# PSUM banks dealt out anew, and weights fetched ahead of their split, in an attention and gated-MLP kernel

## The chip, the cores and the metric

The kernel runs on one core of one Trainium2 chip. The metric is device time in microseconds. Three runs of the kernel before gave 1259.15 us in the median (1252.94 to 1259.8).

## The reference

```
phi(x) = exp(h - max(h)) / sqrt(m),   h = x @ omega.T - sum(x*x)/2      (x scaled by D**-0.25)
kv  = phi(k).T @ v                z = sum over s of phi(k)
x   = (phi(q) @ kv) / (phi(q) @ z + 1e-6)        per batch and head; 8 x 8 heads, 576 rows, D = 64, m = 128
x   -> [4608, 512]                               heads side by side
g   = x @ w_gate;  val = x @ w_val               [4608, 1536] each
out = (silu(g) * val) @ w_out                    [4608, 512]
```

The inputs are float32 (the weights come as 8-byte floats and are converted in the kernel).

## The kernel before, in words

**Precision.** Every matrix of the second half (the MLP, "MoE" in the names) is split into a rounded part and a remainder (`hi` and `lo`, `whi` and `wlo`). A product is three matmuls: hi x hi, hi x lo, lo x hi. ScalarE (ACT) writes the rounded part, VectorE (DVE) or GpSimd (POOL) the remainder.

**Attention, in steps.** 72 steps, each with two groups of 256 rows for a pair of heads (at first keys only, then one query and one key group, at the end two query groups). What a step n does, by function, with the tile that each writes:

- `st_transpose(n + 1)`: four TensorE transposes of the loaded rows `nat` into the PSUM tile `pt` (L373); POOL squares `nat` into `sq` (L380); ACT copies `pt` to `x` (L381).
- `st_project(n)`: `x` times omega into two PSUM tiles `pp`, one for each head of the pair (L396).
- `st_max(n)`: DVE sums the squares (L407), takes the two maxima over `pp` (L414) and makes the bias in two small instructions (L416, L417). The sums are taken ahead of time, some three steps before the maxima of the same step, but stand in the same queue.
- `st_exp(n)`: eight ACT exponentials from `pp` with that bias into `ph` (L428).
- `k_accumulate`: `ph` times `v` into `kvacc` (L530). `q_transpose`: four transposes of a query's `ph` into `ptq` (L554), copied by ACT to `qt` (L556). `q_mult` (batches 0 to 3): `qt` times kv into `po` (L571), normalised by DVE. `q_out`: the result into the PSUM tile `xt` (L604 by transposes, L611 by matmuls), from where ACT copies it, either as `xo` to DRAM (L626) or as the MLP's `xh` with the remainder `xl` by DVE (L632, L633).

**The order of the work.** A list of functions is called for each step: `CLOSE` for steps 0 to 24, `GROUPED` for 25 to 75. Where `GROUPED` has `SHARE`, a stretch of the MLP's work is put in, and of the conversion of the weights (`convert_all`: five DVE instructions for each of 36 pieces, L265 to L273, tiles `st` and `wc`). A scheduler then orders the instructions of each engine by its own estimate of times; each engine and the DMA queue (SP) work strictly in the order that it fixed.

**PSUM.** Eight banks: pool `ps_m` has 4 (MLP tiles `g`, `v`, `o`, and some of the early attention), `ps_p` 2 (`pp`, and besides them `pt` and `xt`), `ps_a` 1 (`ptq`, `po`, `zp`) and `ps_k` 1 (`kvacc`). In the grouped steps `pt` of step n + 1 thus takes the bank that `pp` of step n leaves, and that is free when the exponentials have read it. After attention the last four become `ps_w`, with 4 banks.

**The MLP.** Tiles 0 to 2 (512 rows each) go through `stream()` beside attention: for three columns at a time gate (`g`, L647), SiLU by ACT (L708), value (`v`, L647), product by DVE (L724), split by ACT (`hh`, L727) and POOL (`hl`, L728), down (`o`, L656), added up in `acc` (L671 ACT, L674 DVE). Tiles 3 to 8 go through `pair_rounds()` after it, two tiles at once with seven products in place of eight (Strassen's scheme): 18 visits, each of 2 x 7 products of six matmuls (L851) with eight downs of six matmuls between them. Products are added up in the PSUM tiles `a`, `c`, `d` of `ps_w`, and ACT copies in between (`late`, L919) and DVE sums (L923) stand between products of one tile. New weights come for most visits: `load_seven` fetches two raw pieces (`wraw`, three buffers) from the DRAM scratch `wscr` (L822), DVE forms four sums `s` (L827 to L830), ACT and POOL split them (L841, L842); `load_weights` does it for the down weights (L297, L245, L246). Both start the fetch and the split at the same place of the program.

Of the kernel before, what the change touches and what calls it, by code (L numbers as in the profile page):

```python
# [11 lines left out]
F32 = mybir.dt.float32  # L12
# [11 lines left out]
def kernel(  # L24
# [11 lines left out]
    nc = tc.nc  # L36
# [46 lines left out]
    moe = ctx.enter_context(tc.tile_pool(name="moe", bufs=2))  # L83
    accp = ctx.enter_context(tc.tile_pool(name="accp", bufs=12))
    dram = ctx.enter_context(tc.tile_pool(name="dram", bufs=1, space=DRAM))
    ps_m = ctx.enter_context(tc.tile_pool(name="ps_m", bufs=4, space=PSUM))
    late = ExitStack()
    att = late.enter_context(tc.tile_pool(name="att", bufs=2))
    ps_p = late.enter_context(tc.tile_pool(name="ps_p", bufs=2, space=PSUM))
    ps_a = late.enter_context(tc.tile_pool(name="ps_a", bufs=1, space=PSUM))  # L90
    ps_k = late.enter_context(tc.tile_pool(name="ps_k", bufs=1, space=PSUM))

    ident = const.tile([P, P], F32, name="ident")
# [1 line left out]

    def ps_att(name, shape):
        return ps_a.tile(shape, F32, name=name, tag="b")

    def ps_proj(name, shape):
        return ps_p.tile(shape, F32, name=name, tag="pp")  # L100
# [189 lines left out]
        while (f, i) not in converted:  # L290
            tick()

    def load_weights(f, i, pool=None, tag=None):
        need(f, i)
        new_weights(f, i, pool, tag)
        raw = moe.tile([P, DM], F32, name=f"wraw{f}_{i}", tag="wraw", bufs=3)
        nc.sync.dma_start(raw, wscr[f, i])  # L297
        split_piece(f, i, raw)

# [66 lines left out]
    def st_transpose(n):  # L366
        if n >= NS:
            return
        nat = nats.pop(n)
        pt = (ps_moe if n <= EARLY else ps_proj)(f"pt_{n}", [P, 2, G])  # L370
        for i in range(2):
            for c in range(CH):
                nc.tensor.transpose(  # L373
                    pt[:, i, c * P : (c + 1) * P], nat[:, i, c].rearrange("p h d -> p (h d)"), ident
                )
# [4 lines left out]
        nc.gpsimd.tensor_tensor(sq, nat, nat, op=ALU.mult)  # L380
        nc.scalar.copy(x, pt)  # L381
        sts[n] = x, st, sq
        return True
# [161 lines left out]
    def q_transpose(n):  # L545
        m = n
        todo = [(b, g) for _, b, g, gr in slots(n - TLAG, "q") if b < BPOOL]
        todo += [(b, g) for _, b, g, gr in slots(n - NLAG, "q") if b >= BPOOL]
        for b, g in todo:
            ph = box.pop(("q", b, g))  # L550
            pt = (ps_moe if m < EARLY else ps_att)(f"ptq{b}_{g}", [P, 2, G])
            for hh in range(2):
                for c in range(CH):
                    nc.tensor.transpose(pt[:, hh, c * P : (c + 1) * P], ph[:, c, hh * M : (hh + 1) * M], ident)  # L554
            qts[b, g] = att.tile([P, 2, G], F32, name=f"qt{b}_{g}", tag="qt")
            nc.scalar.copy(qts[b, g], pt)  # L556

    def q_mult(n):
# [36 lines left out]

    def q_out(n):
        n -= OLAG
        for _, b, g, gr in slots(n, "q"):
            po = (ps_att if n + OLAG < EARLY else ps_proj)(f"xt{b}_{g}", [P, G])
            first = column(b, gr)  # L600
            if b < BPOOL:
                xn = xns.pop((b, g))
# [80 lines left out]
    def stream():  # L683

        todo = []
        for vi, (j, s_, k_) in enumerate(visits):
# [24 lines left out]
                for f in fs:  # L711
                    load_weights(nxt[1] * FA + f - fs[0], 0)
            if final:
                load_seven((0, 0), 0)
            while todo:
                down(*todo.pop(0))
                yield MM2
# [12 lines left out]
                if new_set:  # L730
                    load_weights(nxt[1] * FA + f - fs[0], 1)
            if final:
                load_seven((0, 0), 1)
            wts = {f: weights[f, 2] for f in fs} if vi else None
            then = range(nxt[1] * FA, nxt[1] * FA + FA) if new_set else (0, 1) if final else None
            todo = [(j, k_, ht, wts, then, tt) for tt in range(w // P)]
        yield from pair_rounds(todo)

# [76 lines left out]
    def load_seven(key, i):  # L815

        win = late_pools["win"]
        raws_ = []
        r, pf = key
        for f in (2 * pf, 2 * pf + 1):  # L820
            raw = moe.tile([P, DM], F32, name=f"wraw{f}_{i}_{r}", tag="wraw", bufs=3)
            nc.sync.dma_start(raw, wscr[f, i])  # L822
            raws_.append(raw)
# [37 lines left out]
    def pair_rounds(todo):  # L861
# [20 lines left out]
        def one_down():  # L882
            next(prep, None)
            if todo:
                down(*todo.pop(0))
                return True

        for vi, (r, k_, pf) in enumerate(pair_visits):
            then = pair_visits[vi + 1] if vi + 1 < len(pair_visits) else None
            new_w = then and then[2] != pf  # L890
# [18 lines left out]
            for i, use in ((0, gate), (1, value)):  # L909
# [15 lines left out]

                a, c, d = (ps_w.tile([P, T], F32, name=f"{e}{vi}_{i}", tag="w") for e in "acd")
                for n in ORDER:
                    product({5: c, 3: c, 2: d}.get(n, a), n, wts, n in (1, 5, 2))
                    if n == 1:
                        copy("m1", a)  # L930
# [34 lines left out]
    def give(us):  # L965
# [115 lines left out]
```

## Time and profile before

| what | value |
|---|---|
| median of three runs | 1259.15 us |
| the profiled execution's own time | 1259.16 us |
| its span in the trace | 1257.4 us |
| mean granted TensorE clock | 0.973 |
| first matmul of the pairs' visits | 692.7 us after the start of the span |

In the views, PE is TensorE's matmuls and PEld its weight loads. A row of the waits reads "engine and line that waited <- engine and line that ended it: us in total, times, longest". A row of the order of time reads "start, duration, engine, line, operation, out<-in, count [idle before it <- what ended it]". A row of windows gives for each stretch the busy time of each engine with the number of its instructions, then the granted clock and the DMA's share. A step is named by its `pp`: step 47 begins with the projections `pp_47`.

### The profile page before, as it was taken

What the parts mean: (1) busy time and instruction counts of PE and PEld (TensorE: products, weight loads), DVE (VectorE), ACT (ScalarE), POOL (GpSimd) and SP (SyncE); (2) the same over time, 40 slices, a digit from 0 to 9 for tenths busy, and PEclk for the clock granted to TensorE, in tenths of its full rate; (3) what the DMA queues carried; (4) which work ended last, traced back from release to release, by engine and by line L of the source; (5) the groups of instructions that cost most, each with busy time, mean ns of one, the idle gap of its engine ahead of it and who ended that gap; (6) DMA issues with size and microseconds to landing.
All of it is one profiled execution on the core that took longest, in us unless ns stands there. A gap on an engine that the chain in (4) does not pass through costs nothing. (4 is left out here: it accounts for less than half of the span.)

```text
span 1257.4 us, 19064 instructions
## 1 busy us (share of the span) xinstructions
PE 1184.7 (94%) x6633; PEld 968.2 (77%) x6633; DVE 718.8 (57%) x1338; ACT 670.2 (53%) x1503; POOL 608.3 (48%) x515
## 2 busy tenths in 40 slices
PE   6999999989899798998999889999999999999998
PEld 5888777867778576675778778888778888888886
DVE  4788776363765748545527454555744546535544
ACT  3878774656566465465634444444454444454431
POOL 3343333241645747457524456663556662555641
PEclk7999998999899998999999999999999999999999
DMA  5556545352453435222034411112411220412102
GB/s 144 139 141 148 153 132 158 90 151 72 121 140 101 127 92 146 65 73 72 23 111 115 132 62 51 51 51 77 117 42 51 59 60 17 109 51 58 53 17 68
DMA packets 173968, 114.33 MB, mean 91 GB/s; under 512 B 125840, under 2 KB 144304, under 8 KB 173872
## 3 DMA queue, kind: packets, MB, share of 16 engines
q1 hardware_dynamic: 173872, 113.11, 33.0%
q8 instruction: 53, 0.87, 0.3%
q14 instruction: 43, 0.35, 0.1%
HBM read 87.88 MB, written 25.18 MB: 90 GB/s over the span
## 5 line engine op out<-in xcount | busy, mean ns | idle before, releaser
L428 ACT ACTIVATE ph<-pp,st 128x128 f32<-128x128 f32 x576 | 158.3, 386 | 76.2 <-DVE st L417 75.9
L380 POOL TENSOR_TENSOR sq<-nat 128x512 f32<-128x512 f32 x72 | 78.4, 1089 | 141.4 <-DMA nat<-in_k_dram 82.2
L674 DVE TENSOR_TENSOR acc<-o,acc 128x512 f32<-128x512 f32 x156 | 106.6, 684 | 69.8 <-PE o L656 69.8
L842 POOL TENSOR_TENSOR wlo<-wraw,whi 128x512 fp32r<-128x512 f32 (+1 forms) x64 | 66.8, 1043 | 120.5 <-ACT whi L841 119.9
L842 POOL TENSOR_TENSOR wlo<-s,whi 128x512 fp32r<-128x512 f32 x64 | 95.9, 1515 | 57.9 <-ACT whi L841 21.1
L414 DVE TENSOR_REDUCE st<-pp 128x4 f32<-128x512 f32 x144 | 93.6, 683 | 40.9 <-PE pp L396 40.7
L396 PE MATMUL pp<-omT,x 64*128 64x128 f32 x1152 | 102.4, 299 | 1.2 <-ACT x L381 0.4
L396 PEld LDWEIGHTS pp<-omT,x 64*128 64x128 f32 x1152 | 85.0, 198 | 20.9 <-issue 5.4
L246 POOL TENSOR_TENSOR wlo<-wraw,whi 128x512 fp32r<-128x512 f32 x59 | 76.8, 1305 | 40.0 <-ACT whi L245 39.9
L827 DVE TENSOR_TENSOR s<-wraw 128x256 f32<-128x256 f32 x32 | 24.6, 768 | 112.2 <-DMA wraw<-wscr 71.6
L407 DVE TENSOR_REDUCE st<-sq 128x8 f32<-128x512 f32 x72 | 49.1, 681 | 69.0 <-POOL sq L380 69.0
L373 PE MATMUL pt<-ident,nat 128*128 128x128 f32 x288 | 50.9, 299 | 39.1 <-ACT ph L428 36.7
L275 POOL TENSOR_TENSOR wc<-st,wc 128x512 f32<-128x512 f32 x36 | 48.2, 1340 | 73.5 <-DVE wc L273 59.9
L373 PEld LDWEIGHTS pt<-ident,nat 128*128 128x128 f32 x288 | 35.4, 151 | 52.5 <-ACT ph L428 44.5
L656 PE MATMUL o<-whi,late 128*128 128x512 f32 x192 | 74.5, 389 | 0.0
L530 PE MATMUL kvacc<-v,ph 128*128 128x65 f32 x512 | 70.6, 279 | 3.8 <-ACT ph L428 3.3
L530 PEld LDWEIGHTS kvacc<-v,ph 128*128 128x128 f32 x512 | 66.9, 201 | 6.3 <-ACT ph L428 3.6
L919 ACT COPY late<-a 128x512 f32<-128x512 f32 x72 | 42.0, 583 | 50.0 <-PE a L851 47.2
L841 ACT CAST whi<-wraw 128x512 fp32r<-128x512 f32 (+1 forms) x64 | 32.9, 514 | 63.9 <-PE a L851 47.5
L490 POOL TENSOR_TENSOR jk<-ph,zt 128x512 f32<-128x512 f32 x32 | 42.0, 1316 | 48.6 <-ACT ph L428 44.0
L647 PE MATMUL g<-xh,whi 128*128 128x512 f32 x144 | 61.7, 428 | 0.0
L647 PE MATMUL v<-xh,whi 128*128 128x512 f32 x144 | 61.5, 427 | 0.0
(250 smaller groups left out, 3406.0 us busy)
## 6 DMA issues: line engine op xcount, KB each, us to landing
wraw<-wscr SPq DMA_DIRECT2D x123, 256.0 KB, 2.6
wscr<-wc SPq DMA_DIRECT2D x36, 256.0 KB, 2.3
out_dram<-acc SPq DMA_DIRECT2D x72, 128.0 KB, 2.3
nat<-in_k_dram SPq DMA_DIRECT2D x64, 128.0 KB, 3.0
v<-in_v_dram SPq DMA_DIRECT2D x64, 128.0 KB, 3.0
nat<-in_q_dram SPq DMA_DIRECT2D x64, 128.0 KB, 2.6
st<-in_moe_w_gate_dram SPq DMA_DIRECT2D x12, 512.0 KB, 4.9
st<-in_moe_w_val_dram SPq DMA_DIRECT2D x12, 512.0 KB
```

The costliest lines, as they stand in the source:

```text
L246: nc.gpsimd.tensor_tensor(lo, raw, hi.bitcast(F32), op=ALU.subtract)
L373: nc.tensor.transpose(pt[:, i, c * P : (c + 1) * P], nat[:, i, c].rearrange("p h d -> p (h d)"), ident)
L380: nc.gpsimd.tensor_tensor(sq, nat, nat, op=ALU.mult)
L396: nc.tensor.matmul(pp[hh][:, i, c, :], x[r, i, c * P : (c + 1) * P], omT[r], start=True, stop=True)
L407: nc.vector.tensor_reduce(st[:, 0].rearrange("p i c h -> p (i c h)"), sq.rearrange("p i c h d -> p (i c h) d"), axis=AX.X, op=ALU.add,)
L414: nc.vector.tensor_reduce(st[:, 1, :, :, hh], pp[hh], axis=AX.X, op=ALU.max, negate=True)
L428: nc.scalar.activation(ph[:, c, hh * M : (hh + 1) * M], pp[hh][:, i, c, :], AF.Exp, bias=st[:, 3, i, c, hh : hh + 1], scale=1.0,)
L530: nc.tensor.matmul(acc[:, 2 * (pr % 2) + hh, :], ph[:, c, hh * M : (hh + 1) * M], vt[:, 2 * c + j if gr is None else c, hh, :], start=firs ...
L647: nc.tensor.matmul(ps, a_[:, ws], b_[:, c, :], start=n == 0, stop=n == 3 * NC - 1)
L656: nc.tensor.matmul(ps, a_[:, ts_], b_, start=first and n == 0, stop=last and n == 2)
L674: nc.vector.tensor_tensor(a_, po, a_, op=ALU.add)
L842: nc.gpsimd.tensor_tensor(lo, src_, hi.bitcast(F32), op=ALU.subtract)
```

## The change

PSUM: `ps_m` goes from 4 banks to 3, a new pool `ps_b` of one bank takes `pt`, the first `xt` of a step and the second `ptq` of a step; the second `xt` goes to `ps_a`; `ps_p` is left to `pp`. In `GROUPED`, `q_out` moves up behind the first half of `k_accumulate`. `qt` has four buffers in place of two. `ps_w` has five banks. In the pairs' visits a function `weights_work` is called ahead of each product: it fetches (`fetch`) at one product and splits (`make_seven`, or `new_weights` and `split_piece`) at a later one.

```diff
-    ps_m = ctx.enter_context(tc.tile_pool(name="ps_m", bufs=4, space=PSUM))
+    ps_m = ctx.enter_context(tc.tile_pool(name="ps_m", bufs=3, space=PSUM))
...
+    ps_b = late.enter_context(tc.tile_pool(name="ps_b", bufs=1, space=PSUM))
...
+    def ps_tr(name, shape):
+        return ps_b.tile(shape, F32, name=name, tag="t")
...
-        pt = (ps_moe if n <= EARLY else ps_proj)(f"pt_{n}", [P, 2, G])
+        pt = ps_tr(f"pt_{n}", [P, 2, G])
...
-            pt = (ps_moe if m < EARLY else ps_att)(f"ptq{b}_{g}", [P, 2, G])
+            pt = (ps_moe if m < EARLY else ps_tr if i else ps_att)(f"ptq{b}_{g}", [P, 2, G])
...
-            qts[b, g] = att.tile([P, 2, G], F32, name=f"qt{b}_{g}", tag="qt")
+            qts[b, g] = att.tile([P, 2, G], F32, name=f"qt{b}_{g}", tag="qt", bufs=4)
...
-            po = (ps_att if n + OLAG < EARLY else ps_proj)(f"xt{b}_{g}", [P, G])
+            po = (ps_att if n + OLAG < EARLY or i else ps_tr)(f"xt{b}_{g}", [P, G])
...
+        def weights_work(vi, u):
+            r, k_, pf = pair_visits[vi]
+            prev = pair_visits[vi - 1][2] if vi else None
+            fs = (2 * pf, 2 * pf + 1)
+            out_at = 9 if vi == 0 else 2
+            if u == 1 and 1 in coming:
+                make_seven((r, pf), 1, coming.pop(1))
+            if u == out_at and pf != prev:
+                coming[2] = fetch(fs, 2)
+            if u == out_at + 2 and 2 in coming:
+                for f, raw in zip(fs, coming.pop(2)):
+                    new_weights(f, 2, *((accp, "acc") if f % 4 == 3 else ()))
+                    split_piece(f, 2, raw)
+            if vi + 1 < len(pair_visits) and pair_visits[vi + 1][2] != pf:
+                r2, _, pf2 = pair_visits[vi + 1]
+                for i, at in ((0, 5), (1, 12)):
+                    if u == at:
+                        coming[i] = fetch((2 * pf2, 2 * pf2 + 1), i)
+                if u == 8:
+                    make_seven((r2, pf2), 0, coming.pop(0))
...
                 for n in ORDER:
+                    weights_work(vi, unit[0])
+                    unit[0] += 1
                     product({5: c, 3: c, 2: d}.get(n, a), n, wts, n in (1, 5, 2))
...
-                        if new_w:
-                            load_seven((then[0], then[2]), i)
...
-            if new_w:
-                for f in (2 * then[2], 2 * then[2] + 1):
-                    load_weights(f, 2, *((accp, "acc") if f % 4 == 3 else ()))
...
         lambda n: k_accumulate(n, 0),
+        q_out,
         lambda n: k_accumulate(n, 1),
...
-        q_out,
         q_mult,
...
-        ("ps_w", tc.tile_pool(name="ps_w", bufs=4, space=PSUM)),
+        ("ps_w", tc.tile_pool(name="ps_w", bufs=5, space=PSUM)),
```

**TensorE, grouped step 47.** Before, from the last projection of step 47 to the first of step 48 (twelve matmuls for `v_4` and eleven for `v_5` are cut to their first):

```order
L396 MATMUL pp_47_4249<-omT,x_4216 128x128
L554 MATMUL ptq_3_4258<-ident,ph_45_4069 128x128 x4
L530 MATMUL kvacc_1_4059<-v_99,ph_45_4074 128x65 x4
L647 MATMUL v_4_4296<-xh_1236,whi_1_3251 128x512
...
L647 MATMUL v_5_4338<-xh_1236,whi_1_3320 128x512
L373 MATMUL pt_4316<-ident,nat_4026 128x128 x4
L611 MATMUL xt_2_4326<-qt_2_4169,kvr_1_3495 64x256 x2
L647 MATMUL v_5_4338<-xl_1237,whi_1_3320 128x512
...
L396 MATMUL pp_48_4355<-omT,x_4321 128x128
```

The same stretch of TensorE's queue in the changed kernel, whose line numbers are 11 higher here:

```order
L407 MATMUL pp_47_4252<-omT,x_4225 128x128
L565 MATMUL ptq_3_4261<-ident,ph_45_4078 128x128 x4
L541 MATMUL kvacc_1_4068<-v_102,ph_45_4083 128x65 x2
L622 MATMUL xt_2_4270<-qt_2_4172,kvr_1_3507 64x256 x2
L541 MATMUL kvacc_1_4068<-v_102,ph_45_4083 128x65 x2
L658 MATMUL v_4_4305<-xh_1239,whi_1_3256 128x512
...
L384 MATMUL pt_4325<-ident,nat_4029 128x128 x4
L658 MATMUL v_5_4341<-xh_1239,whi_1_3331 128x512
...
L407 MATMUL pp_48_4358<-omT,x_4330 128x128
```

`xt` has moved from behind `pt` to ahead of the MLP's matmuls; the MLP's work between `pt` and the next projections is now a whole group of twelve. On ACT the copy `xo` has moved with `xt`, from behind the exponentials of a step to ahead of them:

```order
L392 COPY x_4225<-pt_4220 128x512
L738 CAST hh_3_4301<-sl_3_4094 128x512
L567 COPY qt_3_4266<-ptq_3_4261 128x512
L637 COPY xo_2_4_4273<-xt_2_4270 128x256
L439 ACTIVATE ph_47_4283<-pp_47_4251,st_4226 128x128 x2
```

Before it read, at the same place of ACT's queue:

```order
L381 COPY x_4216<-pt_4211 128x512
L626 COPY xo_1_4_4224<-xt_1_4221 128x256
L727 CAST hh_3_4292<-sl_3_4085 128x512
L556 COPY qt_3_4263<-ptq_3_4258 128x512
L428 ACTIVATE ph_47_4274<-pp_47_4248,st_4217 128x128 x2
```

So `xo_1` stood behind `x`, and `xo_2` now stands ahead of `ph_47`.

**The DMA queue (SP), first visits of the pairs.** Before, with `wraw_0`, `wraw_1`, `wraw_2` for gate, value and down weights and `out_dram` for finished rows of tile 2:

```order
L297 DMA wraw_2_7663<-wscr 128x512
L678 DMA out_dram<-acc_1_3548 64x512 x2
L678 DMA out_dram<-acc_2_3596 64x512 x2
L822 DMA wraw_1_0_7730<-wscr 128x512
L822 DMA wraw_1_0_7732<-wscr 128x512
L297 DMA wraw_2_7757<-wscr 128x512
```

In the changed kernel:

```order
L307 DMA wraw_2_7678<-wscr 128x512
L689 DMA out_dram<-acc_1_3560 64x512 x2
L689 DMA out_dram<-acc_2_3599 64x512 x2
L307 DMA wraw_1_7715<-wscr 128x512
L307 DMA wraw_1_7717<-wscr 128x512
L307 DMA wraw_2_7789<-wscr 128x512
```

The fetches stand at the same places of the queue as before, in the same order.

More of the change, by code (lines that the diff above doesn't have):

```diff
@@ L291, in need, with load_weights, fetch @@
             tick()
-    def load_weights(f, i, pool=None, tag=None):
+    def load_weights(f, i):
         need(f, i)
[L295 to L298, printed above, removed]
+        fetched = fetch((f,), i)
+        new_weights(f, i)
+        split_piece(f, i, fetched[0])
+    def fetch(fs, i):
+        raws_ = []
+        for f in fs:
+            raw = moe.tile([P, DM], F32, name=f"wraw{f}_{i}", tag="wraw", bufs=3)
+            nc.sync.dma_start(raw, wscr[f, i])
+            raws_.append(raw)
+        return raws_
     omT = const.tile([P, M], F32, name="omT")
@@ L548, in q_transpose @@
         todo += [(b, g) for _, b, g, gr in slots(n - NLAG, "q") if b >= BPOOL]
-        for b, g in todo:
+        for i, (b, g) in enumerate(todo):
             ph = box.pop(("q", b, g))
-            pt = (ps_moe if m < EARLY else ps_att)(f"ptq{b}_{g}", [P, 2, G])
+            pt = (ps_moe if m < EARLY else ps_tr if i else ps_att)(f"ptq{b}_{g}", [P, 2, G])
             for hh in range(2):
@@ L597, in q_out @@
         n -= OLAG
-        for _, b, g, gr in slots(n, "q"):
-            po = (ps_att if n + OLAG < EARLY else ps_proj)(f"xt{b}_{g}", [P, G])
+        for i, b, g, gr in slots(n, "q"):
+            po = (ps_att if n + OLAG < EARLY or i else ps_tr)(f"xt{b}_{g}", [P, G])
             first = column(b, gr)
@@ L713, in stream @@
             if final:
-                load_seven((0, 0), 0)
+                make_seven((0, 0), 0, fetch((0, 1), 0))
             while todo:
@@ L732, in stream @@
             if final:
-                load_seven((0, 0), 1)
+                make_seven((0, 0), 1, fetch((0, 1), 1))
             wts = {f: weights[f, 2] for f in fs} if vi else None
-            then = range(nxt[1] * FA, nxt[1] * FA + FA) if new_set else (0, 1) if final else None
+            then = range(nxt[1] * FA, nxt[1] * FA + FA) if new_set else None
             todo = [(j, k_, ht, wts, then, tt) for tt in range(w // P)]
@@ L813, in split_x, with make_seven @@
         nc.vector.tensor_tensor(lo, ahead[name], hi.bitcast(F32), op=ALU.subtract)
-    def load_seven(key, i):
+    def make_seven(key, i, raws_):
         win = late_pools["win"]
-        raws_ = []
         r, pf = key
[L820 to L823, printed above, removed]
         (a11, a12), (a21, a22) = ((x[:, 0:G], x[:, G:DM]) for x in raws_)
@@ L886, in one_down @@
                 return True
+        coming = {}
+        def weights_work(vi, u):
[18 more added lines that the diff above has]
+                    make_seven((r2, pf2), 0, coming.pop(0))
         for vi, (r, k_, pf) in enumerate(pair_visits):
+            unit = [0]
             then = pair_visits[vi + 1] if vi + 1 < len(pair_visits) else None
-            new_w = then and then[2] != pf
             new_x = then and then[0] != r
```

## The prediction

> **What bounds the kernel now.** I read the page, then windows by stage, then TensorE's waits, then one step in order of time.
>
> ```profile
> span 1257.4 us, 19064 instructions
> PE 1184.7 (94%) x6633; PEld 968.2 (77%) x6633; DVE 718.8 (57%) x1338; ACT 670.2 (53%) x1503; POOL 608.3 (48%) x515
> ```
>
> TensorE is busy 94% of the span and no other engine above 77%, so a gain has to come out of the 73 us in which TensorE stands still, or out of time at a lower clock. The windows show where that is:
>
> ```profile
> core 0: us, PE busy (x) PEld busy (x) DVE busy (x) ACT busy (x) POOL busy (x), PEclk, DMA share, GB/s
> 212.00:640.00 428.00, 388.29 (x2449) 304.55 (x2450) 237.79 (x477) 247.85 (x615) 221.32 (x190) 0.94 0.36 99
> 640.00:692.70 52.70, 52.70 (x255) 42.83 (x254) 29.66 (x44) 22.49 (x40) 15.96 (x13) 1.00 0.42 117
> 692.70:745.00 52.30, 45.23 (x189) 36.01 (x188) 29.43 (x42) 23.68 (x43) 28.72 (x23) 0.97 0.35 103
> 745.00:1240.00 495.00, 492.83 (x2172) 407.04 (x2171) 260.24 (x402) 228.61 (x400) 258.64 (x202) 1.00 0.20 55
> ```
>
> The grouped steps (212 to 640) lose 39.7 us to waits at a clock of 0.94; in the pairs' visits 7.1 us go in the first 52 us and 2.2 us in the next 495. The waits of TensorE, first from 132 to 640 us, then (the last three rows) from 640 us on:
>
> ```profile
> PE pt L373 <- ACT ph L428: 36.7, 20, 4.5
> ...
> PE a L851 <- ACT late L919: 4.9, 3, 3.5
> PE a L851 <- DVE sl2k L923: 2.6, 1, 2.6
> PE o L656 <- POOL hl1k L907: 1.0, 1, 1.0
> ```
>
> One line carries the grouped stage: the transposes `pt` of the next step wait for the exponentials of this one, because they take a bank that `pp` holds. Step 47 in order of time shows what the exponentials wait for:
>
> ```profile
> 368.19 1.16 PE L396 MATMUL pp<-omT,x 64*128 64x128 f32 x16
> 369.28 0.62 SPq L331 DMA_DIRECT2D nat<-in_k_dram  x1
> 369.38 1.29 DVE L414 TENSOR_REDUCE st<-pp 128x4 f32<-128x512 f32 x2 [0.28 <-PE pp L396]
> 371.99 1.04 POOL L380 TENSOR_TENSOR sq<-nat 128x512 f32<-128x512 f32 x1 [0.89 <-DMA nat<-in_k_dram]
> 373.06 0.69 DVE L407 TENSOR_REDUCE st<-sq 128x8 f32<-128x512 f32 x1 [1.93 <-POOL sq L380]
> 373.66 0.16 DVE L417 SCALAR_TENSOR_TENSOR st<-st 128x8 f32<-128x8 f32 x1
> 373.92 2.17 ACT L428 ACTIVATE ph<-pp,st 128x128 f32<-128x128 f32 x8 [3.35 <-DVE st L417]
> 375.62 0.66 PE L373 MATMUL pt<-ident,nat 128*128 128x128 f32 x4 [1.81 <-ACT ph L428]
> 376.37 0.59 ACT L381 COPY x<-pt 128x512 f32<-128x512 f32 x1 [0.29 <-PE pt L373]
> ```
>
> The projections end at 369.35 and the maxima at 370.67, but the bias is held to 373.66 by a sum of squares (L407) that belongs to a step three ahead, whose rows were still on their way. The exponentials end at 376.09, 6.7 us behind the projections. TensorE had reached `pt` 4.5 us behind them and waited 1.81 us.
>
> **The change, part by part.**
>
> *`pt` off the bank of `pp`.* The exponentials still have to be done before the next projections, which need `pp`'s banks, and the copy `x` still stands behind them on ACT. So the wait doesn't vanish: it moves from `pt` to the next `pp`, behind more work. What that is worth, in step 47: before, `pt` (0.66 us in its row; I take 0.44, since the next matmul starts before the last has drained), `xt` (about 0.3, an estimate) and eleven MLP matmuls came after the released wait. The MLP's pitch comes from the chain of waits:
>
> ```profile
> 917.32 1.36 PE c L851 x6
> ```
>
> Six in 1.36 us are 0.227 each, so eleven are 2.5 us, and 3.24 us of TensorE's work now run ahead of the wait. Against it, `pt` could start 0.47 us before the exponentials ended (375.62 against 376.09), and `x` (0.59 us, and about 0.1 to be handed on) now comes after them on the path: 1.16 us. The net cover is 2.1 us per wait. The five longest of the 20 waits are
>
> ```profile
> 281.13 1.11 PE L373 MATMUL pt<-ident,nat 128*128 128x128 f32 x4 [4.54 <-ACT ph L428]
> 336.23 1.11 PE L373 MATMUL pt<-ident,nat 128*128 128x128 f32 x4 [3.24 <-ACT ph L428]
> 440.39 0.66 PE L373 MATMUL pt<-ident,nat 128*128 128x128 f32 x4 [4.03 <-ACT ph L428]
> 483.35 0.90 PE L373 MATMUL pt<-ident,nat 128*128 128x128 f32 x3 [4.24 <-ACT ph L428]
> 584.69 0.69 PE L373 MATMUL pt<-ident,nat 128*128 128x128 f32 x2 [2.93 <-ACT ph L428]
> ```
>
> Less 2.1 each, 2.4 + 1.1 + 1.9 + 2.1 + 0.8 = 8.3 us are left; the other 15, 17.7 us together, leave next to nothing. In the steps of the first and the third, ACT's changed queue has a table load and a SiLU ahead of `x`:
>
> ```profile
> 281.61 1.28 ACT L708 ACT_TABLE_LOAD   x1
> 673.87 0.59 ACT L708 ACTIVATE sl<-g 128x512 f32<-128x512 f32 x1
> ```
>
> That is 1.87 us twice, 3.7 us. I add 2 us (an estimate) for steps where fewer MLP matmuls stood behind `pt`. So 14 us of waits stay and **22.7 us go**. Bounds: 36.7 us if the exponentials come no later and `x` is never late, none if they fall back by the 2.1 us that are gained.
>
> *The clock.* In ten stretches of the grouped stage the granted clock is 0.50. Asked as windows, the one behind step 47's wait, and the sum of the ten:
>
> ```profile
> 376.40:379.80 3.40, 3.40 (x10) 2.19 (x9) 1.54 (x4) 1.55 (x3) 1.65 (x2) 0.51 0.44 112
> sum 47.60, PE 44.65 PEld 34.14 DVE 20.67 ACT 29.43 POOL 22.66; mean PE 4.47 PEld 3.41 DVE 2.07 ACT 2.94 POOL 2.27
> ```
>
> 44.65 us of work at half the rate would take 22.3 at the full one, so they cost up to 22.3 us, 2.2 each. Eight follow a wait of `pt` of 1.8 us or more, the other two a wait of about 2 us elsewhere. After the change three of the waits stay at about 2 us or above, and the other two are not touched: five of ten go, **11 us** (bounds 0 and 22.3). The Trainium skill (TensorE: Matmul & The Clock Gate, HAM oscillation) has the clock fall only for an idle gap above about 3.4 us. Here 1.81 us was enough, so the measurement decides; by the rule one long wait at most (281 us) would keep its stretch, and the time would come out some 9 us lower.
>
> *Three banks for the MLP in place of four.* No MLP tile waits for its bank now. With three, a tile needs the bank of the third before it. In the rows of before that is late at two places, both in the dense stretch behind attention:
>
> ```profile
> 678.39 0.59 ACT L708 ACTIVATE sl<-g 128x512 f32<-128x512 f32 x1
> ...
> 678.45 0.39 PE L656 MATMUL o<-whi,hh 128*128 128x512 f32 x1
> ...
> 682.53 0.39 PE L656 MATMUL o<-whi,hh 128*128 128x512 f32 x1
> ...
> 682.62 1.88 DVE L674 TENSOR_TENSOR acc<-o,acc 128x512 f32<-128x512 f32 x3
> ```
>
> The second down tile would start at 679.0 in place of 678.45, behind the SiLU that reads its bank, and the fourth at 683.3 in place of 682.53, behind the first of three sums: 0.6 + 0.8 = **1.4 us lost**. The Trainium skill (Perfetto Trace Analysis, Optimizing Tensor Performance) wants independent matmul groups to rotate through different banks, so that one's evacuation lies beside the next one's matmuls; fewer banks for the MLP and a single one for `pt` go against that. The rows put a price of 1.4 us on the MLP's part of it.
>
> *`xt` earlier, with its `xo` ahead of the exponentials.* `pt` now needs `xo` done, a copy half as wide as `x` (0.59 us), and 2.7 us of MLP work lie between `xt` and `pt`: hidden. Only in steps 66 to 71 and behind them, with two queries each, an `xt` comes one MLP matmul behind the `ptq` whose bank it takes; it waits for a copy `qt`, as wide as `x`. Five such steps by some 0.4 us: I put **2 us lost** on that (0 to 4).
>
> *Fetches ahead in the pairs' visits, and a fifth bank for `ps_w`.* The DMA queue has the same fetches at the same places between the same stores. A fetch starts when the queue reaches it and one of three `wraw` buffers is free, wherever the program calls it, so it lands when it did. TensorE's order in the visits is unchanged, and all its waits there stand in front of products that add to a begun tile (for a copy or a sum out of that tile) or of a down: a further bank doesn't shorten those. **Nothing**, bounds 0 and the 9.3 us of the windows (7.1 + 2.2).
>
> **The sum,** against the profiled execution: 1259.2 - 22.7 - 11 + 1.4 + 2 = **1229 us**. Its own time is 1259.16 us, span 1257.4, and the median of the three runs is 1259.15, so nothing is to be converted.
>
> **The rivals.**
>
> *All waits of `pt` go* and their eight stretches of half clock with them: 36.7 + 8 x 2.2 = 54 us, 1205 us. For it: 15 of 20 waits are under 2.4 us, and with a whole MLP group always behind `pt` the rows of the step three ahead are asked for sooner before the maxima. Against it: in the worst steps DVE itself is behind:
>
> ```profile
> 270.09 1.16 PE L396 MATMUL pp<-omT,x 64*128 64x128 f32 x16
> ...
> 271.07 1.37 DVE L267 TENSOR_SCALAR wc<-wc 128x512 int32<-128x512 int32 x1
> 272.48 1.66 DVE L269 SCALAR_TENSOR_TENSOR st<-st,wc 128x512 int32<-128x512 int32 x1
> ...
> 275.71 0.68 DVE L414 TENSOR_REDUCE st<-pp 128x4 f32<-128x512 f32 x1
> ```
>
> The weights' conversion (L267, L269) stands ahead of the maxima of step 38, which start 4.5 us behind the end of their projections (275.71 against 271.25), and the change leaves it there. Chance 0.14.
>
> *The wait only changes its name*, from `pt` to `pp`. In the changed queue of DVE 21 sums of squares of steps 25 to 71 stand right ahead of maxima, where it was 10; each that comes late now holds the maxima too (1.29 us). If with this the exponentials fall back by 2.1 us in the 20 waiting steps, nothing is left of the gain, and all ten stretches stay: 1259 us. Chance 0.15.
>
> *Slower: the single bank of `pt` waits for ACT.* `xo` stands behind `hh` and `qt` on ACT, and `hh` waits for DVE:
>
> ```profile
> ACT hh L727 <- DVE sl L724: 38.3, 19, 5.3
> ```
>
> If `hh` holds `xo` by more than the 2.7 us between `xt` and `pt`, TensorE waits at `pt`, and as the exponentials stand behind the same `hh`, it waits at `pp` again. With a third of those 38.3 us on the path, none of the 36.7 us saved and the clock as before, that is 1259 + 13 = 1272 us. The mean of these waits is 2.0 us, below the point from which it decides. Chance 0.08.
>
> *The fetches do shorten the visits* beside the forecast: 1229 - 9 = 1220 us. Against it stands the queue's order. Chance 0.08.
>
> **How the numbers follow.** The forecast, 1229 with 1214 to 1250 for its own unknowns, has 0.55. Faster by over 0.5% (6.3 us, about what a measurement of this kernel can tell from no change): 0.55 + 0.14 + 0.08 = 0.77. Within it 0.15, slower 0.08. The range runs from 1205, which leaves out half of the first rival, to 1260, which takes in two thirds of the second: 0.07 + 0.05 + 0.08 = 0.20 stay outside.
>
> **What would show it.** Right: the row "pt <- ph" is gone, and a row of `pp` waiting for `ph` or `x` has 10 to 18 us, most of it at the steps of 281, 440 and 483 us; about five stretches of half clock are left; the first product of the pairs starts near 662 us in place of 692.7; the pairs' stage takes as long as before, with the 3.5 us wait near its start. Wrong: `pp` waits 30 us or more, `pt` waits for `xo` or `xl`, rows of `g`, `v` or `o` wait for evacuations by several microseconds, or the pairs' waits are gone.

## The result, and the profile after

The changed kernel takes 1249.72 us in the median of 20 runs (1241.23 to 1259.84), the kernel before 1256.87 in 20 runs beside them (1252.57 to 1265.01). The ratio is 0.9936 with a 95% interval of 0.9919 to 0.9954: 7 to 8 us faster, where 30 were forecast. Two lines of its page, then its windows:

```profile
span 1249.8 us, 18994 instructions
PE 1176.9 (94%) x6633; PEld 968.0 (77%) x6633; DVE 707.1 (57%) x1338; ACT 669.4 (54%) x1503; POOL 608.0 (49%) x515
```

```profile
core 0: us, PE busy (x) PEld busy (x) DVE busy (x) ACT busy (x) POOL busy (x), PEclk, DMA share, GB/s
...
212.00:640.00 428.00, 387.04 (x2488) 308.20 (x2486) 230.00 (x482) 250.67 (x621) 223.13 (x191) 0.94 0.35 97
...
688.10:745.00 56.90, 52.63 (x222) 42.34 (x222) 27.31 (x44) 26.93 (x48) 29.42 (x24) 0.97 0.32 94
745.00:1240.00 495.00, 492.23 (x2170) 406.89 (x2169) 262.22 (x408) 226.90 (x396) 259.30 (x203) 1.00 0.20 56
```

The span is 7.6 us shorter, but TensorE stands still as long as before: 72.9 us now (1249.8 - 1176.9), 72.7 before. In the grouped stage the idle time is 41.0 us (it was 39.7) at the same clock of 0.94. TensorE's waits there, from 212 to 640 us:

```profile
PE pp L407 <- ACT x L392: 24.9, 16, 4.6
PE pt L384 <- ACT xo L637: 8.5, 4, 3.0
PE xt L622 <- ACT qt L567: 2.9, 1, 2.9
PE zp L461 <- ACT kvr L455: 2.8, 2, 2.3
PE xt L615 <- DVE xn L592: 1.1, 1, 1.1
PE pp L407 <- ACT ph L439: 0.5, 1, 0.5
```

The row "pt <- ph" of 36.7 us is gone, as forecast, and the six rows that stand there now add up to 40.7 us, as the four of before did (36.7 + 2.0 + 1.6 + 0.4). One step shows why. Step 48 in order of time, in the kernel before and then in the changed one:

```profile
381.10 1.16 PE L396 MATMUL pp<-omT,x 64*128 64x128 f32 x16
...
381.88 0.68 DVE L407 TENSOR_REDUCE st<-sq 128x8 f32<-128x512 f32 x1
...
382.47 1.28 DVE L414 TENSOR_REDUCE st<-pp 128x4 f32<-128x512 f32 x2
...
384.29 2.18 ACT L428 ACTIVATE ph<-pp,st 128x128 f32<-128x128 f32 x8 [0.77 <-DVE st L417]
...
390.41 1.16 PE L396 MATMUL pp<-omT,x 64*128 64x128 f32 x16
```

```profile
374.42 1.16 PE L407 MATMUL pp<-omT,x 64*128 64x128 f32 x16
...
375.01 1.04 POOL L517 TENSOR_TENSOR ph<-ph,dj 128x512 f32<-128x512 f32 x1 [1.75 <-DVE dj L507]
...
376.01 1.26 POOL L739 TENSOR_TENSOR hl<-sl,hh 128x512 fp32r<-128x512 f32 x1
...
377.24 1.04 POOL L391 TENSOR_TENSOR sq<-nat 128x512 f32<-128x512 f32 x1
...
378.31 0.69 DVE L418 TENSOR_REDUCE st<-sq 128x8 f32<-128x512 f32 x1 [2.85 <-POOL sq L391]
...
378.91 1.28 DVE L425 TENSOR_REDUCE st<-pp 128x4 f32<-128x512 f32 x2
...
380.37 0.60 PE L384 MATMUL pt<-ident,nat 128*128 128x128 f32 x4
...
380.68 2.17 ACT L439 ACTIVATE ph<-pp,st 128x128 f32<-128x128 f32 x8 [3.12 <-DVE st L428]
...
385.17 0.58 ACT L392 COPY x<-pt 128x512 f32<-128x512 f32 x1
...
385.81 1.16 PE L407 MATMUL pp<-omT,x 64*128 64x128 f32 x16 [2.09 <-ACT x L392]
```

Before, a sum of squares stood ahead of the maxima too, but found its squares, and the maxima began 0.2 us behind the projections (382.47 against 382.26). Now DVE waits 2.85 us for POOL's squares, with the maxima behind the sum in its queue; they begin 3.3 us late, the exponentials and `x` follow (between the two ACT has 2.3 us of other work, as it had before), and TensorE stands in front of `pp` for 2.09 us. `pt` was free of all that at 380.37, 5.4 us ahead of the projections that use it, and nothing came of it.

What made the squares late in this step is POOL's own queue: POOL went from `ph` to `hl` and on to the squares without a pause, so it wasn't waiting for their rows.

Over steps 33 to 70 (from each step's last projection row to its first row of maxima, of exponentials, and so on, 38 steps) the means are:

| | kernel before | changed |
|---|---|---|
| maxima start behind the projections | 0.89 us | 2.46 us |
| steps in which that is over 1 us | 14 of 38 | 25 of 38 |
| exponentials end | 6.31 us | 7.44 us |
| next projections start | 9.22 us | 9.29 us |

DVE's row for these sums (`st <- sq`), from 212 to 640 us, before and then after:

```profile
DVE st L407 <- POOL sq L380: 47.0, 25, 5.3
```

```profile
DVE st L418 <- POOL sq L391: 68.7, 31, 4.5
```

Looked up one by one in the trace of the changed kernel, some 34 us of these waits (14 of them) end with squares for which POOL itself had waited for rows from DRAM, and 33 us (16) with squares that POOL began straight behind other work.

### The profile page after: what moved, and what is told of

Its sections match the earlier page's. It is cut to its first block, busy times and chain, and to the rows that moved or that the text cites. A ratio compares the mean times of both kernels' runs of the same rounds, so it can differ in the third digit from the quotient of the medians.

```text
span 1249.8 us, 18994 instructions
## 1 busy us (share of the span) xinstructions
PE 1176.9 (94%) x6633; PEld 968.0 (77%) x6633; DVE 707.1 (57%) x1338; ACT 669.4 (54%) x1503; POOL 608.0 (49%) x515
## 5 line engine op out<-in xcount | busy, mean ns | idle before, releaser
L407 PE MATMUL pp<-omT,x 64*128 64x128 f32 x1152 | 98.5, 303 | 30.8 <-ACT x L392 30.4
L407 PEld LDWEIGHTS pp<-omT,x 64*128 64x128 f32 x1152 | 80.5, 201 | 51.9 <-ACT x L392 39.9
L848 POOL TENSOR_TENSOR wlo<-s,whi 128x512 fp32r<-128x512 f32 x64 | 95.3, 1506 | 49.9 <-DVE late L954 18.7
L833 DVE TENSOR_TENSOR s<-wraw 128x256 f32<-128x256 f32 x32 | 24.9, 778 | 120.0 <-DMA wraw<-wscr 82.7
L541 PE MATMUL kvacc<-v,ph 128*128 128x65 f32 x512 | 76.9, 283 | 3.0 <-ACT ph L439 3.0
L541 PEld LDWEIGHTS kvacc<-v,ph 128*128 128x128 f32 x512 | 71.8, 207 | 9.6 <-issue 5.4
L567 ACT COPY qt<-ptq 128x512 f32<-128x512 f32 x72 | 42.5, 597 | 37.2 <-PE ptq L565 37.0
L505 DVE TENSOR_REDUCE dj<-jk 128x4 f32<-128x512 f32 x36 | 24.6, 683 | 66.1 <-POOL jk L501 57.9
```

What stands on the lines that cost most here:

```text
L407: nc.tensor.matmul(pp[hh][:, i, c, :], x[r, i, c * P : (c + 1) * P], omT[r], start=True, stop=True)
L541: nc.tensor.matmul(acc[:, 2 * (pr % 2) + hh, :], ph[:, c, hh * M : (hh + 1) * M], vt[:, 2 * c + j if gr is None else c, hh, :], start=firs ...
```

## The experiments

Theory 1: the sums of squares, which stand three steps ahead of their own in DVE's queue and wait for squares that aren't there yet (their rows are still on the way, or POOL has not come to them), hold the maxima and with them the exponentials. Theory 2: ACT's own queue holds the exponentials and `x`. Theory 3: the single bank of `pt` is what costs. Theories 4 and 5 come up in the expectations of a_st4 and a_nat4. All ratios are to the kernel before, measured beside each.

| kernel | median, us | ratio, 95% interval |
|---|---|---|
| changed | 1249.72 | 0.9936 (0.9919 to 0.9954) |
| a_st3: three buffers for `st` | 1220.22 | 0.9728 (0.9708 to 0.9747) |
| b_st3: the same in the kernel before | 1238.92 | 0.9873 (0.9854 to 0.9892) |
| a_st4: four buffers for `st` | 1247.20 | 0.9942 (0.9914 to 0.9969) |
| a_st2: two buffers for `st` | 1225.23 | 0.9749 (0.9720 to 0.9779) |
| a_nat4: four buffers for the rows | 1232.60 | 0.9819 (0.9794 to 0.9844) |
| att_only: PSUM part alone | 1251.02 | 0.9967 (0.9939 to 0.9995) |
| pair_only: fetch ahead alone | 1255.36 | 1.0009 (0.9988 to 1.0030) |
| att_st3: a_st3 without the fetch ahead | 1221.78 | 0.9730 (0.9699 to 0.9761) |
| st3_qlate: a_st3, `q_out` at its old place | 1233.50 | 0.9818 (0.9786 to 0.9849) |
| st3_xfirst: a_st3, transposes ahead of the exponentials | 1217.48 | 0.9693 (0.9668 to 0.9717) |
| best: that with four buffers for the rows | 1222.10 | 0.9738 (0.9705 to 0.9771) |
| st3_light: a_st3, part of the conversion left out | 1196.76 | 0.9531 (0.9501 to 0.9561) |

**a_st3, the sums behind the exponentials.** A sum writes the tile `st` of its step. With three buffers it can't be placed ahead of the exponentials of three steps before, so it stands at most two steps ahead of its own, where its squares are ready. In DVE's queue 5 sums stand right ahead of maxima from step 25 on, where it was 21.

```diff
-        st = att.tile([P, 4, 2, CH, 2], F32, name=f"st_{n}", tag="st", bufs=6)
+        st = att.tile([P, 4, 2, CH, 2], F32, name=f"st_{n}", tag="st", bufs=3)
```

> The changed kernel with three buffers for the small tile st in place of six: the sum of squares of step n + 3 can then only be written when the exponentials of step n have read their bias, so it stands in front of the maxima of step n + 1 at the latest two steps ahead of its own, and no longer behind rows that are still on their way. Theory 1 (the waits did not go because DVE's sums of squares, waiting for late rows, hold the maxima and with them the exponentials): the maxima start below 1.3 us behind the projections in the mean of steps 33 to 70 (2.46 in the changed kernel), the row pp <- x falls from 24.9 us to below 13, and the time from 1249.7 to 1230 to 1241. Theory 2 (the exponentials are held by ACT's own queue, and the copy x behind them; the sums only fill time in which DVE would have waited anyway): pp <- x stays above 20 us and the time within 4 us of 1249.7. Theory 3 (the single bank of pt, waiting for xo on ACT, is what costs): pt <- xo stays at 8 us or more and the time within 4 us.

TensorE's two largest rows from 212 to 640 us, and step 48 in order of time:

```profile
PE pp L407 <- ACT x L392: 11.6, 7, 3.4
PE pt L384 <- ACT xo L637: 5.9, 3, 2.5
```

```profile
360.52 1.16 PE L407 MATMUL pp<-omT,x 64*128 64x128 f32 x16
...
361.71 1.29 DVE L425 TENSOR_REDUCE st<-pp 128x4 f32<-128x512 f32 x2 [0.39 <-PE pp L407]
...
364.39 2.18 ACT L439 ACTIVATE ph<-pp,st 128x128 f32<-128x128 f32 x8 [0.72 <-DVE st L428]
...
367.54 0.68 DVE L418 TENSOR_REDUCE st<-sq 128x8 f32<-128x512 f32 x1
...
369.74 1.16 PE L407 MATMUL pp<-omT,x 64*128 64x128 f32 x16
```

The maxima begin as soon as the projections end, the sum comes behind the exponentials and without a wait, and the next projections don't wait. The row "st <- sq" is gone from DVE's waits (the sums wait for exponentials now, 14.6 us in 6 waits), the maxima begin 1.35 us behind the projections in the mean, and "pp <- x" is less than half. The mean of 1.35 us is just above the 1.3 that was expected. That is theory 1; theories 2 and 3 expected no change in the time. The gain, 29.5 us, is above what I had put on it (9 to 20).

**b_st3, the same line in the kernel before.**

```diff
-        st = att.tile([P, 4, 2, CH, 2], F32, name=f"st_{n}", tag="st", bufs=6)
+        st = att.tile([P, 4, 2, CH, 2], F32, name=f"st_{n}", tag="st", bufs=3)
```

> The kernel before with the same three buffers for st. Theory 1: the bias was held by the same sums there (step 47: 3 us), so pt <- ph falls from 36.7 us to 15 to 25 and the time from 1256.9 to 1240 to 1250; it gains less than the changed kernel does, since only 10 sums stood right ahead of maxima. Theory 2: pt <- ph stays above 30 us and the time within 4 us of 1256.9.

```profile
PE pt L373 <- ACT ph L428: 24.9, 17, 4.2
```

The wait falls from 36.7 to 24.9 us and the time by 16.5, to 1 us below the expected range. The sums held the kernel before as well. With the sums out of the way, the change takes it from 1238.92 to 1220.22, that is by 18.7 us; with them in the way, 7.2. Where the 18.7 us lie is told below, with the prediction.

**a_st4, a control.** The same line with four buffers: 21 sums are still right ahead of maxima.

```diff
-        st = att.tile([P, 4, 2, CH, 2], F32, name=f"st_{n}", tag="st", bufs=6)
+        st = att.tile([P, 4, 2, CH, 2], F32, name=f"st_{n}", tag="st", bufs=4)
```

> The changed kernel with four buffers for st in place of six. In DVE's queue 21 sums of squares still stand right ahead of maxima in the steps from 27 on, as with six, most of them three steps ahead of their own. Theory 1 (it is the place of the sums in DVE's queue that three buffers changed): within 4 us of the changed kernel, 1246 to 1254, maxima 2.3 to 2.6 us behind the projections in the mean. Theory 4 (fewer buffers for st help in some other way, for instance by holding DVE's other work back): 1230 to 1243, half way to the 1220.2 of three buffers.

1247.20 us, with the maxima 2.40 us behind the projections. Fewer buffers alone do nothing; the place in the queue does.

**a_st2.** The same line with two.

```diff
-        st = att.tile([P, 4, 2, CH, 2], F32, name=f"st_{n}", tag="st", bufs=6)
+        st = att.tile([P, 4, 2, CH, 2], F32, name=f"st_{n}", tag="st", bufs=2)
```

> The changed kernel with two buffers for st: each sum stands one step ahead of its own, 5 of them right ahead of maxima. Theory 1: with three buffers no sum waits for rows any more, so two can gain nothing: 1216 to 1224. Against it could work that DVE now waits at the sum for exponentials that are less far in the past (those of two steps before in place of three) and holds what stands behind: then 1224 to 1235.

1225.23 us, just inside the second range, though its interval overlaps that of a_st3. No gain, as theory 1 has it; whether there is a small loss can't be told.

**a_nat4, the rows sooner.**

```diff
-        nats[n] = att.tile([P, 2, CH, 2, D], F32, name=f"nat{n}", tag="nat", bufs=3)
+        nats[n] = att.tile([P, 2, CH, 2, D], F32, name=f"nat{n}", tag="nat", bufs=4)
...
-            qts[b, g] = att.tile([P, 2, G], F32, name=f"qt{b}_{g}", tag="qt", bufs=4)
+            qts[b, g] = att.tile([P, 2, G], F32, name=f"qt{b}_{g}", tag="qt", bufs=3)
```

> The changed kernel with four buffers for the rows nat in place of three (and three for qt in place of four, for room). The rows of a step can be asked for a step sooner, but DVE's queue then has the sums four steps ahead of their own instead of three, 17 of them right ahead of maxima. Theory 1 (place in the queue): a sum still waits there for rows that were asked for just before, the maxima start 2 us or more behind the projections, and the time is within 6 us of 1249.7. Theory 5 (three buffers for the rows are too few, wherever the sum stands): the sums find their rows, pp <- x falls below 13 us, and the time is 1222 to 1238.

TensorE's and DVE's largest rows from 212 to 640 us:

```profile
PE pp L407 <- ACT x L392: 20.4, 12, 4.6
```

```profile
DVE st L418 <- POOL sq L391: 57.9, 27, 4.3
```

The waits came out as theory 1 had them: DVE still waits 57.9 us for squares, and the maxima begin 2.13 us late. By the trace the waits that end with POOL's waits for rows fell from 34 to 24 us, while those behind POOL's other work stayed (33 and 32 us): sooner rows help the one and not the other. The time did not come out so: 1232.6, 17 us better, which was theory 5's range. In the stage from step 33 to 71 (the table below) 6 us of it are fewer waits and 10 us fewer stretches at half clock. The rows' lateness has a part of its own, then; how much of the clock's share is due to it and how much to where the waits happened to fall, these runs don't settle, the less as the clock's share varies between profiles (below).

**att_only, pair_only and att_st3, the change's two parts.** att_only is the changed kernel with the pairs' visits as before; att_st3 is that with three buffers for `st`; pair_only has PSUM and `GROUPED` as before. Against the changed kernel, cut to their core, att_only and then pair_only:

```diff
-                    weights_work(vi, unit[0])
-                    unit[0] += 1
...
+                        if new_w:
+                            load_seven((then[0], then[2]), i)
```

```diff
-        pt = ps_tr(f"pt_{n}", [P, 2, G])
+        pt = (ps_moe if n <= EARLY else ps_proj)(f"pt_{n}", [P, 2, G])
...
-        ("ps_w", tc.tile_pool(name="ps_w", bufs=5, space=PSUM)),
+        ("ps_w", tc.tile_pool(name="ps_w", bufs=4, space=PSUM)),
```

> The change's PSUM part alone: the pools (five banks for ps_w among them), pt, ptq, xt and q_out as in the changed kernel, the pairs' visits fetching and splitting as in the kernel before. By the prediction the fetch ahead is worth nothing: 1249.7, within 1.5 us. By the rival that the fetches do shorten the visits, the pairs' waits are back at their 9 us and the time is 1252 to 1254.

> The change's other part alone: the kernel before, with weights fetched and split in the pairs' visits as in the changed kernel, and PSUM as it was (four banks for ps_w). By the prediction 1256.9, within 1.5 us; by the rival that the fetches do shorten the visits 1250 to 1254.

> The changed kernel with three buffers for st, but with the weights fetched and split in the pairs' visits as in the kernel before (five banks for ps_w as in the changed one). If the fetch ahead is worth nothing, as predicted: 1220.2 within 2 us. If it shortens the visits, the waits of the product a are longer by 2 us or more and the time is 1222.5 to 1225.

TensorE's waits from 640 us on in the changed kernel, then in pair_only:

```profile
PE a L857 <- DVE sl2k L954: 3.2, 1, 3.2
PE a L857 <- ACT late L950: 3.2, 2, 2.1
PE c L857 <- ACT late L950: 0.7, 1, 0.7
PE o L667 <- ACT sl L719: 0.2, 1, 0.2
```

```profile
PE a L853 <- ACT late L946: 4.7, 2, 3.5
PE a L853 <- DVE sl2k L950: 2.5, 1, 2.5
PE c L853 <- ACT late L946: 0.7, 1, 0.7
```

The fetch ahead alone is worth nothing that can be told (1.0009, give or take 0.002), and the changed kernel with three buffers doesn't miss it (0.9730 against 0.9728). att_only is 1.3 us behind the changed kernel by the medians and 4 us by the ratios, with intervals that overlap, so that pair of runs by itself doesn't exclude a small gain. The waits in the pairs' visits stand in front of the same products for the same copies and sums.

**st3_qlate, the place of `q_out`.**

```diff
         lambda n: k_accumulate(n, 0),
-        q_out,
         lambda n: k_accumulate(n, 1),
...
         lambda n: st_transpose(n + 1),
+        q_out,
         q_mult,
```

> The changed kernel with three buffers for st, and q_out back at its old place in GROUPED, ahead of q_mult: xt then stands four MLP matmuls behind pt on TensorE and not ahead of it. Theory 3 (the single bank, in which pt waits behind xt for the copy xo, costs what its row says, 5.9 us and a half-clock stretch or two): the row pt <- xo goes, but xt now has to wait for the copy x, which stands behind the exponentials: a row xt <- x of 5 us or more comes in its place, and the time is 1218 to 1228. If xo in front of pt were a pure loss, with nothing in its place: 1211 to 1216.

```profile
PE xt L622 <- ACT x L392: 16.3, 11, 4.4
PE xt L615 <- ACT x L392: 8.7, 4, 3.5
PE ptq L565 <- ACT xo L637: 4.8, 1, 4.8
```

The row "pt <- xo" (5.9 us) goes, and 25 us of `xt` waiting for `x` in the same bank come. Part of them only changed place, as `pp` now waits 1.1 us where it waited 12: the stage from step 33 to 71 is 4.6 us longer than in a_st3. Another 8.5 us lie behind step 71, where `ptq` waits 4.8 us for `xo`. By the ratios it is 11 us slower than a_st3 (0.0090 of 1256), by the medians 13, more than I had expected: the early `q_out` is a needed part of the new dealing, and theory 3 falls.

**st3_xfirst and best.** In GROUPED, with three buffers for `st`; best has the two lines of a_nat4 besides.

```diff
         st_max,
+        lambda n: st_transpose(n + 1),
         st_exp,
...
         lambda n: q_norm(n + 1),
-        lambda n: st_transpose(n + 1),
```

> The changed kernel with three buffers for st, and the transposes of the next step called ahead of the exponentials in GROUPED: the copy x then stands in the midst of ACT's eight exponentials and not behind them, and pt comes earlier among TensorE's MLP matmuls. The row pp <- x (11.6 us in 7 waits with three buffers) becomes pp <- ph and loses the copy's 0.6 us in each: 1214 to 1219. If pt, as it comes sooner behind xt, waits longer for xo (5.9 us in 3 waits), nothing or less than nothing is left: 1220 to 1228.

> Three buffers for st, the transposes called ahead of the exponentials, and four buffers for the rows nat (three for qt). No sum waits for its rows with three buffers for st, so a fourth buffer for the rows can only help where pt itself waits for rows or the copy x comes sooner: 1212 to 1219, where three buffers for st and the early transposes alone had 1217.5.

The largest rows of st3_xfirst from 212 to 640 us:

```profile
PE pt L384 <- ACT xo L637: 11.6, 9, 4.0
PE xt L622 <- ACT qt L567: 3.8, 1, 3.8
PE pp L407 <- ACT ph L439: 1.9, 1, 1.9
```

`pp` hardly waits any more, but `pt` waits 5.7 us more for `xo`. The time is in the first range, by another sum than the one expected there: `pp` lost more than the 0.6 us a wait, and `pt` took much of it. At 1217.48 us this is the fastest version that computes the whole; its interval overlaps that of a_st3 (0.9708 to 0.9747), so the 3 us between them are not certain. The further buffer for the rows adds nothing to it: 1222.10 us is outside the 1212 to 1219 expected.

**st3_light, what is left.** Three of the conversion's DVE instructions are left out, the `yield`s stay.

```diff
-            nc.vector.tensor_scalar(ui, ui, 3, 0x3FFFFFFF, op0=ALU.logical_shift_left, op1=ALU.bitwise_and)
             yield
-            nc.vector.scalar_tensor_tensor(ri, ri, -0x40000000, ui, op0=ALU.bitwise_and, op1=ALU.bitwise_or)
             yield
-            nc.vector.tensor_single_scalar(ui, ri, -0x800000, op=ALU.bitwise_and)
```

> The changed kernel with three buffers for st, leaving out three of the five DVE instructions of the weights' conversion (the shift, the joining of exponent and fraction, and the mask), so the weights are wrong and the time tells only what these instructions hold up. Theory 1, for what is left of the waits with three buffers (the conversion stands ahead of late maxima): the maxima start below 0.9 us behind the projections in the mean (1.35 with them), pp <- x falls from 11.6 us to below 5, and the time from 1220 to 1205 to 1213. If ACT's queue is what is left: pp <- x stays above 9 us and the time above 1216.

```profile
PE pp L404 <- ACT x L389: 12.8, 7, 3.6
```

The maxima begin 0.76 us behind the projections, as expected, and the time falls by 23 us, more than expected. But this row did not fall: seven waits stand there as before. That is the sign named for ACT's queue, though the time is far below what was named with it. In six of the seven a conversion instruction that was kept still stands on DVE ahead of the maxima (steps 43 and 58 among them), and in four (steps 38, 43, 53 and 58) ACT also has a table load and a SiLU, 1.8 us or more, between the exponentials and `x`. The gain lies elsewhere: 11 us of it ahead of step 33, which begins at 198.6 us and not at 209.5. Whether leaving out the whole conversion, or another order on ACT, would remove the seven waits was not tried.

**The stage from step 33 to step 71 in eight of the kernels.** Idle time is the window's length less TensorE's busy time; the clock's share is half of the busy time in stretches at half clock; the rest is what is left.

| kernel | stage | idle | half clock | rest |
|---|---|---|---|---|
| before | 399.0 | 36.7 | 17.5 | 344.8 |
| changed | 399.8 | 40.9 | 21.8 | 337.0 |
| b_st3 | 387.0 | 28.6 | 13.3 | 345.2 |
| a_st3 | 376.9 | 23.8 | 16.0 | 337.1 |
| a_nat4 | 384.6 | 34.7 | 11.6 | 338.4 |
| st3_qlate | 381.5 | 28.1 | 14.2 | 339.2 |
| st3_xfirst | 371.6 | 18.0 | 14.6 | 339.0 |
| st3_light | 364.0 | 18.5 | 9.9 | 335.6 |

Single profiles vary: the stage took 397.8 us in pair_only, which has the order of before, and 396.0 in att_only, which has that of the change. a_st4 and att_only, where 21 sums stand right ahead of maxima as in the changed kernel, have 36.8 and 43.5 us in the column idle and 23.5 and 15.3 in that of the clock, so a difference of a few us in either column of two profiles shows nothing; the rest is steadier (336.1 and 337.1).

## Why the prediction was right in direction and wrong in size

*`pt` off the bank of `pp`, 22.7 us to go.* This step failed. That the wait would move to the next `pp`, behind more work, was right. The net cover of 2.1 us per wait took for granted that the exponentials end when they did. They ended 1.13 us later in the mean, since 21 sums in place of 10 now stood right ahead of maxima, and the waits add up to 40.7 us as before. Counted step by step from step 25 on, the 20 steps that waited 36.7 us at `pt` before still wait 24.1 us at `pt` and `pp`, where 14 were forecast, and 13.0 us have come in steps that did not wait. I had the cause in hand. Step 47 was read rightly (the bias held for a sum of a step three ahead), and the rival "the wait only changes its name" named the 21 sums, at a chance of 0.15. But the sum treated the exponentials' end as fixed, although the diff's new order of DVE bore on it. a_st3 and its control a_st4 show that the sums held the changed kernel.

They don't show that the 22.7 us were there but for the sums. Of the 18.7 us between b_st3 and a_st3, the stage from step 33 to 71 has 10.1 (387.0 to 376.9): some 5 us less idle (att_st3 has 23.9 as well), 8.1 us less of the rest, and a clock's share that is no smaller (13.3 and 16.0). The wait of 24.9 us at `pt` did become one of 11.6 at `pp`, as the step's reasoning has it, but 5.9 us at `pt` for `xo` and some others came beside it. What is left of the 18.7 us lies outside that stage.

*The clock, 11 us to go.* It hung on the first step and fell with it, and it did not come with the sums out of the way either. The eight stretches of the grouped stage are 47.80 us with 43.71 us of TensorE's work in them: 21.9 us, against 22.3 before.

*Three banks for the MLP, 1.4 us lost.* A row "o <- sl" of 0.2 us is all there is. The rule cited there (the Trainium skill, Perfetto Trace Analysis, Optimizing Tensor Performance) has independent matmul groups rotate through different banks; here one bank fewer for the MLP's groups cost 0.2 us.

*`xt` earlier, 2 us lost.* The wait of `xt` for `qt` came (2.9 us, once). What I had taken as hidden, `pt` behind `xo`, was not: 8.5 us in four waits. That is the rival with the single bank, at a smaller price than its 13 us; st3_qlate shows that the other order costs more.

*Fetches ahead, nothing.* Right, as far as can be told: pair_only 1.0009, att_st3 as a_st3.

*What no term held.* In steps 33 to 71 the waits and the clock's cost grew by some 4 us each, and yet the stage is only 0.8 us longer, since TensorE's rest fell by 7.8 us. It did so in each kernel of the table with the new dealing of PSUM (335.6 to 339.2 against 344.8 and 345.2). From one start to the next, waits and half clock taken off, the rows of `pt` follow at 99 ns in place of 131 and those of `pp` at 69 in place of 73. For `pt` much of it is what stands next in TensorE's queue: before, in 32 of the steps (counted in the same way), `xt` started 175 ns behind the start of the last transpose in the mean, while in the changed kernel, in 22 of them, an MLP matmul starts 28 ns behind it. So the new order is part of it; no run parts the order from the bank, nor says what makes the 175 ns. The first pair product comes 4.6 us sooner (688.1), where 662 was forecast; with the variation between profiles, the 7.2 us are not to be divided further.

## What to carry to other kernels

Before costing a freed buffer, ask what sets the time of the work that it waits for, and look at the changed order of that engine's queue: an instruction that was put there early holds everything behind it when its input is late, whether a transfer or another engine's queue makes it so. More buffers let a scheduler put work earlier than its data come, and fewer buffers for one small tile (three in place of six) were worth more here than a PSUM bank. A change that brings little can be worth more with a second obstacle removed (here 18.7 us in place of 7.2), but then too one has to count where the gain came from: only about 5 of the 18.7 us were waits in the stage that the prediction was about.

## What the runs showed of the hardware

The clock goes by a fixed grid. In the fourteen profiles (before, changed, twelve experiments), from 200 to 1190 us, every stretch at half clock is a multiple of 3.41 us long and begins on a grid of that pitch. Four windows on it, of the changed kernel:

```profile
381.62:385.03 3.41, 2.10 (x10) 1.38 (x8) 1.03 (x3) 3.38 (x8) 1.82 (x2) 1.00 0.30 67
385.03:388.44 3.41, 2.63 (x28) 2.08 (x28) 0.87 (x3) 2.37 (x6) 2.12 (x3) 1.00 0.06 14
514.74:518.15 3.41, 0.47 (x4) 0.05 (x3) 0.72 (x2) 3.30 (x10) 1.26 (x1) 1.00 0.71 208
518.15:521.57 3.42, 3.42 (x24) 3.20 (x24) 2.47 (x6) 0.31 (x1) 2.04 (x2) 0.50 0.01 3
```

The wait of 2.09 us before 385.81 falls into two windows, both above 60% busy, and costs no clock; that of 2.94 us before 518.11 leaves one window 14% busy (0.47 of 3.41), and the next runs at half the clock. I cut all fourteen profiles so. Of the windows at full clock, 75 were less than 40% busy, and the next was at half clock in all 75; of 77 between 40 and 60%, in 30; of 3746 above 60%, in one. So standing still for more than 60% of one window (2.05 us) costs about another 1.7 us, half a window (an estimate from these figures), and mostly nothing if it is split over two. The Trainium skill (TensorE: Matmul & The Clock Gate, Part 1) has a free-running window of about 3.4 us, which these traces show, but an idle gap of a whole window as what lowers the clock; here 60% of one was enough.
